# First batch's scale sums as TensorE Gram products, row statistics on ScalarE, idle TensorE slots filled with matmuls, and an offset per operation in the order

## The chip, the cores and the metric

One core of one Trainium2 chip. The metric is the device time of one execution in microseconds (us). The kernel before takes 1000.96 us, the median of three runs (1000.89 to 1001.48).

TensorE is PE in the rows (PEld its weight loads), VectorE is DVE, ScalarE is ACT, GpSimd is POOL, and SyncE is SP, which issues every DMA from one queue.

## The reference

Eight batches of attention with 8 heads, 512 local and 32 global positions of 64 values, then a layer that mixes each batch by a two-dimensional FFT and ends in a feed-forward block:

```python
s_l   = concat([q_l @ k_g.T, where(|i - j| <= 32, q_l @ k_l.T, -1e9)]) / 8
out_l = softmax(s_l) @ concat([v_g, v_l])
out_g = softmax(q_g @ concat([k_g, k_l]).T / 8) @ concat([v_g, v_l])
x  = concat([out_g, out_l]) transposed to (8, 544, 512)
u  = x + real(fft(fft(x, axis=1), axis=2))
un = (u - mean(u)) / sqrt(var(u) + 1e-6)          # over the last axis
out = u + relu(un @ w_ch1) @ w_ch2                # 512 -> 2048 -> 512
```

## The kernel before

The work is cut into jobs. Each `add(engine, us, function, ...)` in `jobs_weights`, `jobs_batch`, `jobs_pair`, `jobs_scores`, `jobs_dft`, `jobs_chunk`, `jobs_mixes` and `jobs_duo` names a job's engine, an assumed length, what it reads and writes, and a due time `t`. The planner `Plan.run` deals the jobs out by due time under the buffers that are free, and `emit` writes them in that order, so that each engine has a fixed list and works through it in order. An engine whose next instruction waits lets nothing behind it pass.

Four kinds of work share the engines:

- **Pairs of heads**, 32 of them, four to a batch (p = 0 to 3 are batch 0). A pair's q, k and v (`load`, `load_v`) are scaled by powers of two that come from sums of their absolute values: `sums` and `sums_v` on ACT, one product with a 128x128 matrix that adds over partitions (`total` in `z_total`), then `z_scale` and `scales` on DVE. `prep_mul` (ACT) scales q and k in place, `prep_hi` (ACT) and `prep_lo` (POOL) split them into two fp16 parts; `v_mul`, `v_hi`, `v_lo` do so for v. Then come, for four units a pair, the scores (PE), a masked copy that also gives the maximum (DVE), exponentials (`exps`) and their two fp16 parts `p_hi` (ACT) and `p_lo` (POOL), a transpose by DMA (`turn`), `values` (PE) and `norm` (DVE), which writes X.
- **The transform of a batch.** `x_square` and `g_square` (ACT) sum the absolute values of X, and `total`, `dft_scale`, `dft_inv` turn that into scales `dsc`. `d_even`, `d_odd` and `d_tail` fold X, and `d_tail_hi`, `d_hi`, `d_lo` split it (tiles ht and eh). `d_first` (PE) is the product along one axis and `d_z`, `d_z2` split its result; `d_second` is the product along the other axis, and `d_add`, `d_addc` and `d_tadd` add it to X.
- **Chunks of 256 rows** through the feed-forward block, c = 0 to 16. `l_bn` takes means and variances, `l_v` turns them into the factors `ve`, `l_hi`, `l_un` and `l_lo` normalise and split, and the rows are turned round: chunk 0 by PE (`l_flip`, 16 matmuls against an identity) and copies (`l_put`) into uh. `f_first` is 24 matmuls of 256 columns, `f_second` 12 of 512.
- **Weights**, 32 loads of 512 KB. `w_low` and `w_split64` and then `w_size` unpack one into a tile, `w_sum` (PE) multiplies its upper halves by themselves, `w_max`, `w_norm` and `w_scale` draw a power of two out of that, and `w_hi` (ACT) and `w_lo` (DVE) split the tile with it.

All weights and all of batch 0, transform and layer norm included, must be through before the first `f_first`. From there on the feed-forward block of one chunk runs while later batches go through attention and transform. Two dictionaries decide what goes first at the start: `FAST` puts batch 0's transform and chunk 0 ahead of other work by a bonus, and `ALOW = 4` gives one `w_low` in four to ACT, the others to POOL.

## Time and profile before

| | before |
|---|---|
| median of three runs | 1000.96 us |
| the profiled execution | 1000.05 us |
| its span, from the first instruction to the last | 998.1 us |
| mean granted TensorE clock over the span | 0.948 |
| PE busy | 906.3 us (91%) |
| DVE, ACT, POOL busy | 725.2, 632.0 and 584.9 us |
| first matmul of the first `f_first` | 139.11 us |

A clock of 1.00 is 2.4 GHz and one of 0.50 is 1.2 GHz. The durations below are from the profiled execution. Busy shares are means over stages that have different limits, so the table alone doesn't say what a change is worth.

### The profile page before, as it was taken

Reading aid. Unit: us, or ns where it says so; the run is one execution under the profiler, and the core shown is the slowest. Engines: PE = TensorE matmul, PEld = TensorE weight load, DVE = VectorE, ACT = ScalarE, POOL = GpSimd, SP = SyncE. Lnnn points to the kernel's source line nnn. Section 1 sums busy time; section 2 is a strip of 40 time slices with the busy share of each in tenths; the row PEclk is TensorE's granted clock in tenths of the full one; section 3 lists DMA queues with packets and bytes.
Section 4 is the critical chain, followed back from the end, with each engine's and each line's share of the span. In section 5 each row is a group of like instructions: output and inputs, shape, how many; then the busy total and the mean of one; then the engine's idle time right before and its main releaser. Section 6 shows DMA issues by size and latency. Waiting matters only on the chain.

```text
span 998.1 us, 24488 instructions
## 1 busy us (share of the span) xinstructions
PE 906.3 (91%) x9352; PEld 631.3 (63%) x9352; DVE 725.2 (73%) x1913; ACT 632.0 (63%) x1353; POOL 584.9 (59%) x860
## 2 busy tenths in 40 slices
PE   1444369999999999999999999999999999999996
PEld 1333347766776767667776676777777666666663
DVE  3788788888757875788578767978775788854543
ACT  6996779967787767666866778576663435421110
POOL 5897468765694658457845875478367266940000
PEclk9665569999999999999999999999999999999998
DMA  9899456735874576368554663668273123201001
GB/s 352 278 254 198 141 128 116 158 98 87 172 141 109 113 132 145 81 134 123 146 95 97 134 165 72 126 115 136 41 130 51 43 51 70 48 6 43 1 1 43
DMA packets 228529, 114.13 MB, mean 114 GB/s; under 512 B 201372, under 2 KB 211004, under 8 KB 228412
## 3 DMA queue, kind: packets, MB, share of 16 engines
q1 hardware_dynamic: 228412, 112.57, 51.3%
q8 instruction: 73, 1.20, 0.5%
q14 instruction: 44, 0.36, 0.1%
HBM read 48.97 MB, written 9.44 MB: 59 GB/s over the span
## 4 chain that ended last, share of the span: by engine, by line
PE 84%; ACT 4%; DMA 4%; DVE 3%; POOL 2%; issue 1%; SPq 1%; DVEq 0%; POOLq 0%; ACTq 0%
PE ps L1088 28%; PE acc L1107 27%; PE bk L1239 7%; PE ps L1306 4%; PE acc L1306 4%; PE bk L632 4%; PE bk L677 2%; PE bk L680 2%; PE bk L959 2%; DMA rw<-in_moe_w_ch 2%; PE bk L924 1%; DMA vf<-in_v 1%; PE bk L706 1%; ACT junk L537 1%; PE bk L742 1%
## 5 line engine op out<-in xcount | busy, mean ns | idle before, releaser
L1088 PE MATMUL ps<-uh,wh 128*128 128x256 f16 x2496 | 290.8, 274 | 0.8 <-ACT uh L1062 0.5
L1107 PE MATMUL acc<-wh,h 128*128 128x512 f16 x1248 | 285.9, 379 | 0.0
L1088 PEld LDWEIGHTS <-wh 128*128 128x128 f16 x2496 | 240.1, 98 | 38.8 <-issue 4.0
L1107 PEld LDWEIGHTS <-h 128*128 128x128 f16 x1248 | 117.1, 98 | 129.7 <-issue 4.4
L656 POOL TENSOR_TENSOR ph<-pe,ph 128x448 f16<-128x448 f32 (+1 forms) x128 | 142.4, 1123 | 82.1 <-ACT ph L651 72.3
L1097 DVE SCALAR_TENSOR_TENSOR h<-ps,h 128x512 f16<-128x512 f32 x104 | 71.5, 687 | 96.9 <-ACT h L1093 96.4
L1093 ACT ACTIVATE h<-ps 128x512 f16<-128x512 f32 x104 | 61.8, 594 | 112.0 <-PE ps L1088 104.4
L647 ACT ACTIVATE pe<-pe,nm 128x224 f32<-128x224 f32 (+1 forms) x256 | 106.1, 475 | 17.5 <-DVE nm L640 17.2
L640 DVE CUSTOM_DVE_ANT_0 pe<-bk,msk,z 128x224 f32<-128x224 f32 (+1 forms) x256 | 101.9, 454 | 12.7 <-PE bk L632 10.4
L651 ACT ACTIVATE ph<-pe 128x448 f16<-128x448 f32 (+1 forms) x128 | 72.2, 579 | 12.1 <-DMA pl<-ph 9.7
L677 PE MATMUL bk<-vN,pl 128*128 128x65 f16 x768 | 64.9, 199 | 7.0 <-DMA pl<-ph 7.0
L677 PEld LDWEIGHTS <-pl 128*128 128x128 f16 x768 | 57.9, 101 | 15.8 <-DMA pl<-ph 10.2
L445 PE MATMUL wl<-wm 128*128 128x128 bf16 x128 | 18.0, 285 | 50.2 <-DVE wm L435 49.2
L618 POOL TENSOR_TENSOR kT<-qk,kT 128x655 f16<-128x655 f32 x32 | 46.3, 1447 | 24.0 <-ACT kT L613 20.7
L680 PEld LDWEIGHTS <-pl 96*128 96x128 f16 (+1 forms) x768 | 55.9, 102 | 3.9
L592 POOL TENSOR_TENSOR vN<-vf,vN 128x640 f16<-128x640 f32 x32 | 45.0, 1406 | 22.5 <-ACT vN L588 11.8
L581 POOL TENSOR_TENSOR vf<-vf,z 128x640 f32<-128x640 f32 x32 | 40.7, 1271 | 22.1 <-DVE ge L543 12.0
L632 PE MATMUL bk<-kT,qT 64*128 64x224 f16 (+2 forms) x960 | 53.4, 255 | 0.3 <-DVE nm L640 0.3
L1288 ACT ACTIVATE hb<-ph 128x512 f16<-128x512 f32 x16 | 10.1, 630 | 66.8 <-DVE ph L1273 66.8
L680 PE MATMUL bk<-vB,pl 96*128 96x65 f16 (+1 forms) x576 | 49.9, 199 | 0.0
L603 ACT ACTIVATE qk<-qk,z 128x655 f32<-128x655 f32 x64 | 46.5, 768 | 0.7 <-DVE z L543 0.7
L537 ACT ACTIVATE junk<-qk 128x512 f16<-128x512 f32 x64 | 43.9, 686 | 3.6 <-DMA qk<-in_qk 2.3
(262 smaller groups left out, 1830.2 us busy)
## 6 DMA issues: line engine op xcount, KB each, us to landing
qk<-in_qk SPq DMA_DIRECT2D x32, 583.5 KB
rw<-in_moe_w_ch SPq DMA_DIRECT2D x22, 512.0 KB
vf<-in_v SPq DMA_DIRECT2D x32, 320.0 KB
out<-X SPq DMA_DIRECT2D x13, 512.0 KB
raw<-in_moe_w_ch SPq DMA_DIRECT2D x10, 512.0 KB
vB<-vN SPq DMA_DIRECT2D x96, 32.5 KB
vB<-vN SPq DMA_DIRECT2D x32, 65.0 KB
pl<-ph SPq DMA_TRANSPOSE x128
```

The lines of the kernel that those rows point to most:

```text
L632: nc.tensor.matmul(S[h][:, t + w0:t + w1], qT[r, a, j], kT[r, KW * c + k0:KW * c + k0 + w1 - w0], start=m == 0, stop=m == 2)
L640: nc.vector.tensor_tensor_reduce(self.per[j][:, h, 0:w], S[h][:, t:t + w], self.msk[:, j, 0:w], z[:, 8:9], 3e38, op0=ALU.add, op1=ALU.min, ...
L647: self.nc.scalar.activation(pe[:, h], pe[:, h], AF.Exp, bias=nm[:, h:h + 1], scale=-1.0)
L651: self.nc.scalar.activation(ph[:, 0, :, 0:WIDE[i % 4]], self.per[i % 4][:, :, 0:WIDE[i % 4]], AF.Copy)
L656: self.nc.gpsimd.tensor_sub(ph[:, 1, :, 0:w], self.per[i % 4][:, :, 0:w], ph[:, 0, :, 0:w])
L677: nc.tensor.matmul(pv[:, j % 2, h], pl[:, 4 * a + 2 * h], vN[:, j, c, h, :], start=m == 0, stop=False)
L680: nc.tensor.matmul(pv[:, j % 2, h], pl[0:n, 4 * a + 2 * h + 1], vb, start=False, stop=m == 2)
L1088: nc.tensor.matmul(ps[:, q], wt[:, w, c0:c0 + P], uh[:, :, 4 * a + kt, :], start=n == 0, stop=n == 11)
L1097: self.nc.vector.scalar_tensor_tensor(h[:, 1], self.fps.pop((c, fp)), 0.0, h[:, 0], op0=ALU.max, op1=ALU.subtract)
L1107: nc.tensor.matmul(self.acc_f[c][j], h[:, a, q, j * P:(j + 1) * P], self.w[1, f][:, w, :], start=f == 0 and a == 0 and w == 0, stop=f == 1 ...
L1239: nc.tensor.matmul(ps, w[x], a[:, :, k * y + o + kt, :], start=m == 0, stop=m == 5)
L1306: nc.tensor.matmul(self.acc_f[c][j], h[:, a, q, j * P:(j + 1) * P], self.w[1, f][:, w, :], start=first and q + a + w == 0, stop=last and q ...
```

## The change

Seven edits, of which the last moves work on all engines.

1. For batch 0 the sums of absolute values on ACT go. `gram` multiplies the upper halves of q, k and v by themselves on PE, 15 matmuls of 128 columns for each of the four pairs, and `gram_max` (DVE) takes the largest entry of each row; `root_of` draws the scale from that, as `w_scale` does for the weights.
2. For pairs 0 and 2 (`DIRECT`) the scaling pass goes: ACT's `prep_hi` and `v_hi` scale while they round, and DVE's `low_of` takes over the low parts of k, q and v from POOL.
3. `ALOW = 2`: every second `w_low` is ACT's. Four `w_lo` go from DVE to POOL in two steps each (`LOP`).
4. The first two operations of `l_v` go from DVE to ACT; the third stays on DVE as `l_m`.
5. `warm` jobs, matmuls of 512 columns on constants whose result nobody reads, are planned from 99 us on wherever PE has nothing else, up to the first `f_first`.
6. Chunk 0's first `l_flip` writes to another PSUM buffer, the last weight sum takes a bank, batch 0's `d_tail` another scratch tile, and `f_first` no longer waits for the end of all weight sums.
7. `OFF`, 149 numbers, is added to due times by operation and by batch, and the planner's constants change.

```diff
+DIRECT = (0, 2)
+OFF = {
+        "b0b_hi": -19.9, "b0b_lo": 2.0, "b0b_mul": -1.2, "b0b_sum": -4.5, "b0d_add": 9.5, "b0d_addc": -2.3, "b0d_first": 9.4, "b0d_hi": -2.1,
...
-ALOW = 4
-LOP = ()
+ALOW = 2
+LOP = (6, 14, 29, 31)
-WARM = ()
-L_HOLD = 81.469
+WARM, WARM_AT = 130, 99.125
+L_HOLD = 105.291
...
+    def gram(self, p):
+        s, pb = self.st[p], self.bank(("bank", "gm", p))
+        for n, f in enumerate((s["q"], s["k"], s["vf"].rearrange("p a b d -> p (a b d)"))):
+            f = f.bitcast(BF16).rearrange("p (n t) -> p n t", t=2)[:, :, 1]
+            at = [*range(0, f.shape[1] - P, P), f.shape[1] - P]
+            for i, o in enumerate(at):
+                self.nc.tensor.matmul(pb[:, P * n:P * n + P], f[:, o:o + P], f[:, o:o + P], start=i == 0, stop=i == len(at) - 1)
...
+        self.nc.vector.tensor_reduce(self.acc[p // 2 % 2][:, n:n + 3], pb, axis=EX, op=ALU.max)
...
+    def root_of(self, r, v):
+        ve, r = self.nc.vector, r.bitcast(I32)
+        ve.tensor_scalar(r, v.bitcast(I32), -0.5, RSQRT, op0=ALU.mult, op1=ALU.add)
+        ve.tensor_scalar(r, r, EXPO, None, op0=ALU.bitwise_and)
...
+    def low_of(self, lo, f, s, hi):
+        self.nc.vector.scalar_tensor_tensor(lo, f, s, hi, op0=ALU.mult, op1=ALU.subtract)
...
-        nc.vector.tensor_scalar(v, mv[:, :, 1], 1e-6, 1.0 / 16.0, op0=ALU.add, op1=ALU.mult)
-        nc.vector.tensor_scalar(y.bitcast(I32), v.bitcast(I32), -0.5, 1597463007.0, op0=ALU.mult, op1=ALU.add)
-        nc.vector.scalar_tensor_tensor(ve[:, 2], mv[:, :, 0], -1.0, y, op0=ALU.mult, op1=ALU.mult)
+        nc.scalar.activation(v, mv[:, :, 1], AF.Copy, scale=1.0 / 16.0, bias=1e-6 / 16.0)
+        nc.scalar.activation(y.bitcast(I32), v.bitcast(I32), AF.Copy, scale=-0.5, bias=1597463007.0)
+
+    def l_m(self, c):
+        mv, ve = self.L[c]["mv"], self.L[c]["ve"]
+        self.nc.vector.scalar_tensor_tensor(ve[:, 2], mv[:, :, 0], -1.0, ve[:, 1], op0=ALU.mult, op1=ALU.mult)
...
     def warm(self, n):
-        self.nc.tensor.matmul(self.bank(("bank", "wm", n)), self.c1[:, 0, 0, 0:P], self.c2.rearrange("p a b c d -> p (a b c d)")[:, 0:512], start=True, stop=True)
+        if n == 0:
+            self.wps = self.ps.tile([P, 512], F32, name="wps", tag="acc1")
+        self.nc.tensor.matmul(self.wps, self.c1[:, 0, 0, 0:P], self.c2.rearrange("p a b c d -> p (a b c d)")[:, 0:512], start=True, stop=True)
...
+        for n in range(WARM):
+            add("PE", .24, self.warm, n, r=[("const",)] + ([] if n else [("ws", 1, 1)]), t=1e6, hold=WARM_AT, margin=.05)
...
-            add("PE", 2.65, self.f_first, c, fp, r=[uh, ("wend",)] + w1, w=[ps], t=t, back=False, margin=.3)
+            add("PE", 2.65, self.f_first, c, fp, r=[uh] + w1, w=[ps], t=t, back=False, margin=.3)
...
+            j.t += OFF.get(j.tag + n, 0.0)
```

What the planner makes of it shows in the engines' lists. Ahead of the first `f_first` PE's list grows from 722 matmuls to 903: 60 of `gram`, 109 of `warm`, and 12 scores that stood behind it; behind it the lists hold the same matmuls but for those scores. Three places matter below.

On ACT, at batch 0's transform, before: L802 is the last x_square and L794 g_square, L537 are sums of batch 1, five of them ahead of the first split of the transform (L897 is d_tail_hi, L874 d_hi).

```order
L783 ACTIVATE X<-xg 32x64 x4
L537 ACTIVATE junk,vac_68<-qk 128x512
L802 ACTIVATE junk,vax_70<-X 128x256
L794 ACTIVATE junk,vax_70<-xg 128x128
L537 ACTIVATE junk,vac_68<-qk 128x655
L537 ACTIVATE junk,vac_68<-vf 128x640
L537 ACTIVATE junk,vac_68<-qk 128x512
L537 ACTIVATE junk,vac_68<-qk 128x655
L897 ACTIVATE ht<-et,dsc 32x513 x2
L874 ACTIVATE eh<-e_1281,dsc 128x514
```

The same place now (L448 and L455 unpack the last weight, L864 is x_square, L856 g_square, L959 d_tail_hi, L936 d_hi, L579 the sums):

```order
L845 ACTIVATE X<-xg 32x64 x4
L448 ACTIVATE ps_1451<-rw 128x512
L448 ACTIVATE ps_1477<-raw 128x512
L455 ACTIVATE lw<-raw 128x512
L864 ACTIVATE junk,vax_70<-X 128x256
L856 ACTIVATE junk,vax_70<-xg 128x128
L959 ACTIVATE ht<-et,dsc 32x513 x2
L936 ACTIVATE eh<-e_1317,dsc 128x514
L579 ACTIVATE junk,vac_68<-qk 128x512
L579 ACTIVATE junk,vac_68<-qk 128x655
```

The sums of batch 1 moved behind the two splits, and the unpacking of the last weight now stands between the copies of the global rows and x_square.

On DVE, from the layer norm's statistics to the first copy into uh, before (L1023 to L1025 are `l_v`, L1030 `l_un`, L1040 `l_lo`, L985 `d_addc`, L1060 `l_put`; masked copies L640 left out):

```order
L1018 BN_AGGR mv<-bst 128x2
L1023 TENSOR_SCALAR ve<-mv 128x2
L1024 TENSOR_SCALAR ve<-ve 128x2
L1025 SCALAR_TENSOR_TENSOR ve<-mv,ve 128x2
L1030 TENSOR_SCALAR un<-X,ve 128x512 x2
L1040 TENSOR_TENSOR unh<-un,unh 128x512 x2
...
L985 SCALAR_TENSOR_TENSOR X<-bk_121,dsc,X 128x2x128 x4
L976 SCALAR_TENSOR_TENSOR X<-bk_123,dsc,X 128x2x128 x2
L1060 COPY uh<-bk_122 128x512
```

And now (L1047 is `d_addc`, L1090 `l_m`, L1054 `d_tadd`, L1125 `l_put`; masked copies L702 left out):

```order
L1080 BN_AGGR mv<-bst 128x2
L1047 SCALAR_TENSOR_TENSOR X<-bk_122,dsc,X 128x2x128 x4
L1090 SCALAR_TENSOR_TENSOR ve<-mv,ve 128x2
L1095 TENSOR_SCALAR un<-X,ve 128x512 x2
L1105 TENSOR_TENSOR unh<-un,unh 128x512 x2
...
L1125 COPY uh<-ps_1857 128x512
L1054 SCALAR_TENSOR_TENSOR xt<-bk_123,dsc,xt 32x2x128 x4
L1125 COPY uh<-flt 128x512
```

Two of `l_v`'s rows are ACT's now, four `d_addc` moved ahead of the third, and four `d_tadd` stand between the two copies.

On PE, from batch 0's last values to `d_first`, before (L472 is `total`, of batch 0's X and of batch 1's first sums; L924 `d_first`):

```order
L680 MATMUL bk_123<-vN,pl 128x65
L472 LDWEIGHTS parth
L472 MATMUL bk_122<-vax_70,parth 128x7
L472 LDWEIGHTS parth
L472 MATMUL bk_121<-vac_68,parth 128x7
L924 LDWEIGHTS eh
L924 MATMUL bk_124<-c1r,eh 128x144
```

And now (L1422 is `warm`; 12 of them stand ahead of the `total`, and 28 between it and `d_first`, L986):

```order
L1422 MATMUL wps<-c2r,c1r 128x512
L497 LDWEIGHTS parth
L497 MATMUL bk_121<-vax_70,parth 128x7
L1422 LDWEIGHTS c1r
L1422 MATMUL wps<-c2r,c1r 128x512
...
L986 LDWEIGHTS eh
L986 MATMUL bk_122<-c1r,eh 128x144
```

The second `total` moved behind the even half of `d_first`, and the fillers came in front of `d_first` instead. Further runs of them stand before `d_second` (11 and 5, then 13), before the scores and `l_flip` (16 and 6) and before the last scores (8). On SP the last weight's load now stands behind the last transposes of batch 0 instead of ahead of them.

## Rows read from the trace of the kernel before

**Rows 1.** Windows by stage: start:end, length, busy us of each engine, clock, DMA share.

```profile
0.00:139.74 139.74, 57.66 (x723) 42.28 (x724) 101.46 (x286) 113.90 (x239) 98.98 (x135) 0.66 0.78 232
...
250.00:360.00 110.00, 110.00 (x1274) 77.94 (x1271) 83.07 (x242) 84.14 (x183) 74.89 (x115) 1.00 0.66 132
...
690.00:800.00 110.00, 110.00 (x1178) 78.37 (x1177) 81.01 (x212) 57.58 (x116) 56.26 (x81) 1.00 0.36 64
```

**Rows 2.** Waits of PE after 139 us: total, times, longest.

```profile
PE ps L1088 <- ACT uh L1062: 0.5, 1, 0.5
```

**Rows 3.** Windows of the stage ahead of the first f_first.

```profile
70.00:90.00 20.00, 11.79 (x203) 9.11 (x203) 18.18 (x55) 18.78 (x43) 18.00 (x23) 0.62 0.75 163
90.00:100.00 10.00, 2.72 (x33) 2.14 (x33) 6.84 (x19) 2.95 (x7) 5.59 (x9) 0.50 1.01 226
```

**Rows 4.** Timeline of SP's queue: start, length, line.

```profile
93.81 6.13 SPq L661 DMA_TRANSPOSE pl<-ph  x2
```

**Rows 5.** Timeline of ACT, with the idle time before a row in brackets.

```profile
98.85 0.62 ACT L422 ACTIVATE ps<-rw 128x512 f32<-128x512 f32 x1 [3.40 <-DMA rw<-in_moe_w_ch]
...
104.25 0.63 ACT L537 ACTIVATE junk<-qk 128x512 f16<-128x512 f32 x1 [1.90 <-DMA qk<-in_qk]
```

**Rows 6.** Groups of ACT to 106 us, shapes apart: busy, mean ns, idle before.

```profile
L429 ACT ACTIVATE lw<-rw 128x512 int32<-128x512 uint32 x6 | 3.9, 652 | 0.0
...
L603 ACT ACTIVATE qk<-qk,z 128x655 f32<-128x655 f32 x4 | 3.3, 828 | 0.0
...
L537 ACT ACTIVATE junk<-qk 128x655 f16<-128x655 f32 x4 | 3.0, 752 | 0.1
...
L537 ACT ACTIVATION_READ_ACCUMULATOR junk<-qk 128x1 f32 x9 | 1.7, 187 | 0.0
```

**Rows 7.** Groups of DVE to 139.7 us, shapes apart.

```profile
L481 DVE SCALAR_TENSOR_TENSOR wh<-wm,wsc,wh 128x512 f16<-128x512 f32 x18 | 18.2, 1021 | 4.0 <-ACT wh L488 4.0
...
L711 DVE TENSOR_REDUCE ng<-bk 128x1 f32<-128x497 f32 x2 | 1.3, 664 | 0.0
```

**Rows 8.** Timeline of DVE: w_scale's first row, last norm, dft_inv, d_lo.

```profile
103.41 0.16 DVE L456 TENSOR_SCALAR mx<-wl 128x1 int32<-128x1 int32 x1 [0.40 <-PE wl L451]
...
105.21 0.42 DVE L693 TENSOR_TENSOR X<-bk,dn 128x256 f32<-128x256 f32 x1
...
108.94 0.15 DVE L546 TENSOR_SCALAR dsc<-dsc 128x1 int32<-128x1 int32 x1
...
113.14 0.75 DVE L878 SCALAR_TENSOR_TENSOR eh<-e,dsc,eh 128x514 f16<-128x514 f32 x1 [0.75 <-ACT eh L874]
```

**Rows 9.** Timeline of ACT: d_tail_hi of batch 0.

```profile
110.89 1.47 ACT L897 ACTIVATE ht<-et,dsc 32x513 f16<-32x513 f32 x2
```

**Rows 10.** Timeline of PE: the total ahead of d_first.

```profile
113.88 0.17 PE L472 MATMUL bk<-vac,parth 128*128 128x7 bf16 x1 [6.99 <-ACT junk L537]
```

**Rows 11.** Timeline of DVE: l_v's first two rows, last l_put, chunk 1's l_v.

```profile
128.75 1.10 DVE L1023 TENSOR_SCALAR ve<-mv 128x2 f32<-128x2 f32 x1
129.88 1.17 DVE L1024 TENSOR_SCALAR ve<-ve 128x2 int32<-128x2 int32 x1
...
139.27 0.42 DVE L1060 COPY uh<-flt 128x512 f16<-128x512 f16 x1
...
141.54 0.17 DVE L1024 TENSOR_SCALAR ve<-ve 128x2 int32<-128x2 int32 x1
```

**Rows 12.** Timeline of PE: first f_first, then scores.

```profile
139.74 4.29 PE L1088 MATMUL ps<-uh,wh 128*128 128x256 f16 x23 [0.26 <-DVE uh L1060]
143.97 0.75 PE L632 MATMUL bk<-kT,qT 64*128 64x224 f16 x12
```

**Rows 13.** Timeline of PE: a later f_first and an f_second.

```profile
157.65 2.79 PE L1088 MATMUL ps<-uh,wh 128*128 128x256 f16 x24
...
161.05 2.76 PE L1107 MATMUL acc<-wh,h 128*128 128x512 f16 x12
```

**Rows 14.** Window of half a microsecond in the first f_first.

```profile
143.50:144.00 0.50, 0.50 (x7) 0.27 (x7) 0.00 (x0) 0.00 (x0) 0.00 (x0) 1.00 1.04 236
```

More of the change, by code (lines that the diff above doesn't have):

```diff
@@ L281, in run @@
             j.start = s
+            going = going or j.fn.__name__ == "f_first"
+            if going and j.fn.__name__ == "warm":
+                j.us = 0.0
             free[e] = s + j.us
@@ L1400, in jobs_scores @@
             x = .05 if nm == "k" else 0
+            if p in DIRECT:
+                add("ACT", .55 + x, self.prep_hi, p, nm, r=[z, o, qk], w=[d])
+                add("DVE", .75 + 4 * x, self.prep_lo, p, nm, r=[z, o, qk, d], w=[d])
+                continue
             add("ACT", .63 + x, self.prep_mul, p, nm, r=[z, o, qk], w=[o])
@@ L1484, in jobs_dft @@
         et, ht = ("et", b), ("ht", b)
[L1485 removed]
+        add("POOL", 4.1, self.d_tail, b, r=xtg, w=[et, ("un" if b else "unh", "st", b)], k=[xt])
         eh = [("eh0", b), ("eh1", b)]
@@ L1525, in jobs_chunk @@
             add("DVE", .86, self.l_bn, c, j, r=r0[j:j + 1], w=[("mv", c)], k=[X], t=L, back=LNB)
-        add("DVE", 1.05, self.l_v, c, r=[("mv", c)], w=[ve], t=L, back=LNB)
+        add("ACT", .40, self.l_v, c, r=[("mv", c)], w=[ve], t=L, back=LNB)
+        add("DVE", .50, self.l_m, c, r=[("mv", c), ve], w=[ve], t=L, back=LNB)
         for j in range(2):
@@ L1579, in jobs_duo @@
                 add("DVE", .86, self.l_bn, c, j, r=[("uj", c, j)], w=[("mv", c)], k=[X], t=L, back=False)
-            add("DVE", 1.05, self.l_v, c, r=[("mv", c)], w=[ve], t=L, back=False)
+            add("ACT", .40, self.l_v, c, r=[("mv", c)], w=[ve], t=L, back=False)
+            add("DVE", .50, self.l_m, c, r=[("mv", c), ve], w=[ve], t=L, back=False)
         end = [("xM", 31), ("xgo", 7, 1)]
```

144 lines of the change are left out of this document (85 added, 59 removed), and 19 rows, old and new, of the table OFF.

## The prediction

> **What bounds the kernel now.** I read the windows by stage first. From the first `f_first` on PE has no gap: its busy time equals the length of the five windows from 250 to 800 us (110.00 of 110.00 in the first and the last of them) at full clock [rows 1], and the longest wait that PE shows after 139 us is 0.5 us [rows 2]. So the span is three pieces laid end to end: the time to the first `f_first` (139.11 us, in the table), some 849 us of matmuls that nothing holds up, and a short end. A cheaper operation on DVE, ACT or POOL after 139 us gives nothing. A microsecond off the first piece is a microsecond off the whole.
>
> In the first piece PE is busy 57.7 of 139.7 us and the other three 99 to 114 [rows 1]. Until 90 us they are nearly full: 18.2, 18.8 and 18.0 of 20 us from 70 to 90, with the DMA at 0.75 of full; from 90 to 100 they drop to 6.8, 3.0 and 5.6 while the DMA stands at 1.01 [rows 3]. That is two limits in turn, work first and then transfers. SP hands over batch 0's last two transposes at 93.81 and is held 6.13 us by them [rows 4]; ACT waits 3.40 us for a weight at 98.85 and then 1.90 us for batch 1's first q and k [rows 5]. The last norm of batch 0 ends at 105.21 + 0.42 = 105.63 [rows 8], which I call N. From N to the first `f_first` there are 33.5 us in which one engine waits for the next, and the clock on PE is at its half level: 0.50 from 90 to 100 [rows 3] and still 23 matmuls in 4.29 us in the first `f_first`, where later 24 take 2.79 [rows 12, 13].
>
> **The change, part by part.** I sum against the profiled execution, 1000.05 us, and add the 0.91 us by which the median lies above it.
>
> **A, work ahead of N.** ACT loses twelve sums at 0.75 + 0.19 us (the rows of a sum overlap a little: 10 us in all) and four scalings (0.83 for k, by columns 0.65 for q: 3.0) and takes seven `w_low` at 0.65 (4.6) [rows 6], so 8.4 us less. POOL loses low parts, some products and eight `w_low`. DVE gains. Four `gram_max` of 384 columns cost 0.51 each by 0.664 us for 497 columns [rows 7]. `low_of` costs between 0.75 us for 514 columns with POOL idle [rows 8] and 1.02 us for 512 in the same form while POOL works [rows 7]; over eight calls of 655, 512 and twice 320 columns for two pairs that is 5.3 to 7.2 us. Four `w_lo` (4.1) and the last `w_scale` (eight rows like the 0.16 us at 103.41 [rows 8], 1.3) leave it. DVE thus has 2.0 to 3.9 us more ahead of N, and was at 18.2 of 20 in the densest window. PE's 60 extra matmuls are hidden: it was busy under half of this piece.
>
> The 1.02 us against 0.75 us is one place where the Trainium skill speaks against this change. "SBUF — State Buffer", section "Who interferes with whom", says that a VectorE instruction with two SBUF inputs contends with a GpSimd instruction that reads SBUF. `low_of` has two such inputs, and by that rule all eight calls would cost the upper figure; the rows agree with it in the one pair of durations.
>
> What does N gain? At least nothing: the same bytes go through the same queue, and transfers were the last limit. At most about 8.4 us, ACT's relief, if transfers could all move up. The DMA's own slack caps that: a quarter of the 20 us from 70 to 90, 5.0 us, is room for transfers that come earlier [rows 3]. On top of it `w_scale` no longer stands ahead of the last norm, and the last weight changes places with the last transposes, which brings the transposes forward but puts that weight's unpacking ahead of the last x_square on ACT. Between 0 and 8.4 I take **-4.0**, near the DMA's slack, less 1 us for DVE's extra work.
>
> **B, from N to the first f_first.** Step by step:
> - *To d_first.* Before, it follows a `total` at 113.88 for which PE had waited 6.99 us because of batch 1's sums [rows 10], so at N + 8.25. Now `d_tail_hi` follows `dft_inv`, which ends at 108.94 + 0.15 = N + 3.46 [rows 8]; 1.47 for the tail [rows 9], half of that for `d_hi`, 0.75 for `d_lo` [rows 8] make N + 6.4. But fillers stand in PE's list: 12 ahead of the `total`, 28 behind it. One is 2.76 / 12 = 0.23 us at full clock [rows 13], and twice that at half. The first 12 can start about when the last norm does. The clock rose between 139.11 and 143.5 when PE had no gap (1.00 at 143.5 [rows 14]), so I take the 12 at mixed speed to N + 3.6 and the 28 at 0.23, 6.4 us, to N + 10.0. That is 1.75 us later than before. `d_first`'s first 24 matmuls of 144 columns then take 1.44 us in place of 2.88, worked out from the two clock levels. Sum +0.3; bounds -3.3 (fillers hidden) and +8.4 (all 40 at half clock, with `d_first` too: N + 18.1 less 8.25, and 1.4 back where the wait was for other engines).
> - *The odd half* of `d_first`, 16 matmuls, at full clock: -1.0; bounds 0 and -1.5 with `d_second`.
> - *w_scale* moves here, onto DVE ahead of `d_add` and the statistics: +1.3; nothing if DVE waits there anyway.
> - *l_v.* Its first two rows take 1.10 and 1.17 us [rows 11] where the same line takes 0.17 in chunk 1 [rows 11]. Now ACT has them, and DVE does four `d_addc` of 256 columns meanwhile, some 1.7 us by half of 0.75 and a little. -0.6 if that sets the pace, +1.0 if ACT's list, which holds batch 1's splits ahead of `l_v`, is late. I take -0.3.
> - *To the last copy into uh*, which started at 139.27 [rows 11]: between the two halves' low parts and that copy DVE now has the masked copies, one copy and four `d_tadd`; before there were also four `d_addc` and four `d_add` in place of the `d_tadd`. Four rows fewer, 0.4 us each, less what ACT's three sums cost its own copies: -1.2; bounds 0 and -1.7.
>
> Together **-0.9**, bounds -5 and +8.
>
> On `l_v` the Trainium skill speaks against the change a second time: "ScalarE: Activation LUTs", section "Rules for kernel authors", says to use VectorE rather than ScalarE for add and multiply, and to budget about 0.3 us for each activation. By that, two would cost an estimated 0.6 us against 0.34 on a VectorE that nothing disturbs, and the sum would be 0.3 us less good; the 1.10 and 1.17 us of the trace outweigh it in this one place, where the time counts.
>
> **C, the first f_first at full clock.** Its 24 matmuls ran from 139.11 to the scores at 143.97, 4.86 us; later ones take 2.79 [rows 12, 13]. With fillers up to the last moment: **-2.1**, and nothing if the clock falls before it.
>
> **D, twelve scores** (0.75 us [rows 12]) move from behind the first `f_first` to ahead of it, where PE has time: **-0.75**.
>
> Behind that nothing is removed from PE: 0. All matmuls there are the same, in another order. What covers it is the room that the other engines have (83 of 110 us on DVE, 84 on ACT [rows 1]); without that cover, every late operand is a gap.
>
> Sum: -4.0 - 0.9 - 2.1 - 0.75 = -7.75 on 1000.05, so 992.3, and by the median 993.2 us, **0.8% faster**.
>
> **The rivals.**
> 1. *N doesn't move.* The transfers were the last limit at 90 to 100 us [rows 3], their bytes are unchanged, and DVE gets more work. Then A is nothing or at most the 0.6 us of `w_scale`, and the time is 993.2 + 3.6 = 996.8. Against it: ACT was at 18.8 of 20 when the DMA had a quarter free. Chance 0.24.
> 2. *The fillers become the bound (slower).* A filler is not skipped when real work is ready. If the clock stays at half through the 40 around the `total`, they last 18.4 us where about 6.7 are free, `d_first` starts at N + 18.1, and C is lost with it: B is +8, so -4.0 + 8 - 0.75 = +3.3, 1004.2. It decides from the point where B passes +4.8. For it: 0.50 in every window of this stage. Against: the clock did rise within 4.4 us of matmuls without a gap. Chance 0.09.
> 3. *PE gets gaps behind 143 us.* New due times move every operation, and one chunk's un or one batch's transposes arriving late shows as a wait where there was 0.5 us. The engines' lists have room in the mean, but order decides. To eat the gain takes 7.75 us of gaps; a few us, hence about 998, are likelier than that. Chance 0.13, of which a third slower than before.
> 4. *Both limits ahead of N give way* and B comes to its good bound: -8 - 3 - 2.9, about 987. Chance 0.08.
>
> My own forecast, 990 to 996, has 0.46. Changes under 0.2% (2 us) can't be told from none here. Slower than that: most of rival 2 and a third of rival 3, 0.13. Same: 0.08, from what is left of rivals 1 to 3 near 1000. Faster: 0.79. The range that leaves 2 in 10 out is 987.0 to 1000.5 us.
>
> **What the new profile would show.** Right, if the last norm ends near 101.6, the granted clock is 1.00 before the first `f_first`, this starts near 134.2 and its 24 matmuls take under 3 us, and the windows behind stay at 110.00 of 110.00. A is wrong if ACT waits longer for weights or DVE's row before the last norm is late on `low_of`; B is wrong if PE runs fillers while eh or z is long ready; C is wrong if the clock is 0.50 at `f_first`. PE waits after 140 us that sum to more than 1 us would show rival 3.

## The result, and the profile after

The changed kernel takes 1006.15 us (median of five runs, 1005.04 to 1008.21) against 1000.96 for the kernel before (five runs beside them, 998.63 to 1001.48): a ratio of 1.0057 [1.0039, 1.0074]. It is **slower by 0.6%**, where 0.8% faster was predicted, and lies outside the range. The span of the profiled execution grew by 6.4 us, from 998.1 to 1004.6.

The stage ahead of the first `f_first` did get shorter. Windows of the changed kernel by the same stages as [rows 1], the first up to the first `f_first`:

```profile
0.00:136.03 136.03, 83.59 (x903) 55.58 (x903) 105.96 (x296) 106.35 (x217) 85.12 (x121) 0.84 0.83 237
250.00:360.00 110.00, 109.66 (x1279) 77.14 (x1277) 87.17 (x243) 83.13 (x186) 75.01 (x110) 1.00 0.72 136
690.00:800.00 110.00, 110.00 (x1148) 78.37 (x1147) 72.77 (x200) 49.15 (x106) 33.89 (x57) 1.00 0.31 62
```

`f_first` starts 3.08 us earlier, POOL is down from 99 to 85 us of this stage, and the two long windows behind are nearly as full as before (109.66 and 110.00 of 110). Here is the start itself, in the timeline of PE (compare [rows 12]):

```profile
136.03 5.41 PE L1153 MATMUL ps<-uh,wh 128*128 128x256 f16 x48
```

48 matmuls in 5.41 us are 2.7 per 24: full clock from the first one. What the predicted gain went into shows in the waits of PE behind this point. The kernel before had one of 0.5 us there [rows 2], and two of 0.3 and 0.2. The four longest now (total, times, longest):

```profile
PE acc L1172 <- DVE wh L506: 3.0, 2, 2.4
PE ps L1371 <- DVE hb L1358: 1.9, 1, 1.9
PE bk L694 <- POOL qT L680: 0.9, 1, 0.9
PE bk L694 <- POOL kT L680: 0.7, 1, 0.7
```

The first, third and fourth lie together, at 157 to 168 us; the second is one wait at 864 us. Where time was gained and lost, I read from the two traces with a count of my own: the columns of the matmuls that each kernel still has ahead of it at one and the same time (fillers left out), divided by 2.4 GHz, so in us at full clock. The difference is how far the changed kernel is ahead of the one before. It is good to about 1 us.

| at (us) | 145 | 155 | 160 | 165 | 170 | 175 | 300 | 860 | 880 | end |
|---|---|---|---|---|---|---|---|---|---|---|
| ahead by (us) | 6.5 | 6.0 | 4.9 | 2.1 | -2.1 | -3.4 | -2.9 | -4.3 | -6.4 | -6.3 |

6.5 us were won by 145 us. 9.4 of what was lost went within 20 us, from 155 to 175, and 2.1 at 864. Windows of the first place (in the kernel before PE is busy 5.00 of 5 in each of these four, at clock 1.00):

```profile
155.00:160.00 5.00, 4.46 (x37) 2.24 (x36) 4.21 (x7) 5.00 (x11) 4.88 (x7) 1.00 0.70 143
160.00:165.00 5.00, 3.39 (x33) 1.38 (x30) 5.00 (x1) 2.34 (x6) 5.00 (x5) 0.77 0.57 133
165.00:170.00 5.00, 2.60 (x7) 0.93 (x7) 4.93 (x12) 2.50 (x7) 1.79 (x2) 0.50 1.02 242
170.00:175.00 5.00, 5.00 (x102) 3.84 (x101) 3.85 (x16) 4.12 (x9) 3.02 (x6) 0.71 0.40 47
```

PE is idle for 4.55 of the 20 us, and its clock falls to 0.50: its busy time in each window by what the clock lacks of 1.00 is 0.78 + 1.30 + 1.45 = 3.5 us more. DVE shows one single instruction in the second window. The timeline of DVE has it, the low half of the sixth second-layer weight:

```profile
158.81 0.85 DVE L506 SCALAR_TENSOR_TENSOR wh<-wm,wsc,wh 128x512 f16<-128x512 f32 x1
159.89 7.45 DVE L506 SCALAR_TENSOR_TENSOR wh<-wm,wsc,wh 128x512 f16<-128x512 f32 x1 [0.23 <-ACT wh L513]
```

And POOL at that time, a row without a gap, the low parts of pairs 6 and 7 (L680) and of two units' p (L718):

```profile
159.78 1.42 POOL L680 TENSOR_TENSOR kT<-qk,kT 128x655 f16<-128x655 f32 x1
161.17 1.15 POOL L680 TENSOR_TENSOR qT<-qk,qT 128x512 f16<-128x512 f32 x1
162.28 2.02 POOL L718 TENSOR_TENSOR ph<-pe,ph 128x448 f16<-128x448 f32 x2
164.26 1.42 POOL L680 TENSOR_TENSOR kT<-qk,kT 128x655 f16<-128x655 f32 x1
165.65 1.14 POOL L680 TENSOR_TENSOR qT<-qk,qT 128x512 f16<-128x512 f32 x1
```

The same instruction takes 0.74 us when nothing disturbs it, and 0.78 to 1.86 in the kernel before between 150 and 176. Here it lasts 7.45 us and ends at 167.34, 0.55 us behind POOL's row. `f_second` needs that half and waits 2.41 us; all that is queued behind it on DVE waits too, and ACT waits 5.0 us for this `w_lo`.

### The profile page after: what moved, and what is told of

The parts are those of the page before. It is cut to its first block, busy times and chain, and to the rows that moved or that the text cites. A ratio compares the mean times of both kernels' runs of the same rounds, so it can differ in the third digit from the quotient of the medians.

```text
span 1004.6 us, 24794 instructions
## 1 busy us (share of the span) xinstructions
PE 935.2 (93%) x9521; PEld 645.5 (64%) x9521; DVE 722.4 (72%) x1890; ACT 630.0 (63%) x1367; POOL 577.8 (58%) x852
## 5 line engine op out<-in xcount | busy, mean ns | idle before, releaser
L1172 PE MATMUL acc<-wh,h 128*128 128x512 f16 x1248 | 288.5, 381 | 3.0 <-DVE wh L506 3.0
L718 POOL TENSOR_TENSOR ph<-pe,ph 128x448 f16<-128x448 f32 (+1 forms) x128 | 139.8, 1100 | 98.3 <-ACT ph L713 85.4
L702 DVE CUSTOM_DVE_ANT_0 pe<-bk,msk,z 128x224 f32<-128x224 f32 (+1 forms) x256 | 102.4, 454 | 11.3 <-PE bk L694 10.9
L680 POOL TENSOR_TENSOR kT<-qk,kT 128x655 f16<-128x655 f32 x30 | 43.3, 1444 | 16.8 <-ACT kT L672 15.3
L694 PEld LDWEIGHTS <-qT 64*128 64x128 f16 x960 | 36.4, 99 | 16.1 <-issue 10.9
L645 POOL TENSOR_TENSOR vN<-vf,vN 128x640 f16<-128x640 f32 x30 | 41.8, 1395 | 7.9 <-ACT vN L637 7.0
L1371 PE MATMUL ps<-wh,hb 128*128 128x512 f16 x192 | 44.2, 379 | 1.9 <-DVE hb L1358 1.9
L1371 PE MATMUL acc<-wh,h 128*128 128x512 f16 x192 | 45.8, 379 | 0.0
```

Source lines behind the costliest of these rows:

```text
L694: nc.tensor.matmul(S[h][:, t + w0:t + w1], qT[r, a, j], kT[r, KW * c + k0:KW * c + k0 + w1 - w0], start=m == 0, stop=m == 2)
L702: nc.vector.tensor_tensor_reduce(self.per[j][:, h, 0:w], S[h][:, t:t + w], self.msk[:, j, 0:w], z[:, 8:9], 3e38, op0=ALU.add, op1=ALU.min, ...
L718: self.nc.gpsimd.tensor_sub(ph[:, 1, :, 0:w], self.per[i % 4][:, :, 0:w], ph[:, 0, :, 0:w])
L1172: nc.tensor.matmul(self.acc_f[c][j], h[:, a, q, j * P:(j + 1) * P], self.w[1, f][:, w, :], start=f == 0 and a == 0 and w == 0, stop=f == 1 ...
L1371: nc.tensor.matmul(self.acc_f[c][j], h[:, a, q, j * P:(j + 1) * P], self.w[1, f][:, w, :], start=first and q + a + w == 0, stop=last and q ...
```

## The experiments

Each ratio is against runs of the kernel before beside it; "ahead" is the count of the table, from the profiled execution. Where a kernel has "the tail of before", this is its diff (by itself it brings 1006.15 down to 1003.77, see below, so kernels with it compare with that):

```diff
-PL = 75
-T_AT, T_PACE = 803.116, 12.26
-BOOST = 0
+PL = 39.601
+T_AT, T_PACE = 793.534, 12.914
+BOOST = 12.091
```

### Is it the long w_lo? (pause, no low halves, clock)

**A pause on GpSimd.** POOL's next low part has to wait for that `w_lo`, by a copy of two of its columns:

```diff
+            if at in (("prep_lo", 6, "q"), ("p_lo", 22)):
+                held.append(j)
                 continue
             j.fn(*j.a)
+            if at == ("w_lo", 1, 5, False):
+                k.nc.gpsimd.tensor_copy(k.rest, k.w[1, 5][:, 1, 0:2])
+                for h in held:
+                    h.fn(*h.a)
```

> Changed kernel with one added wait: ahead of the second low part of pair 6 (prep_lo of q), GpSimd first reads two columns that w_lo of the sixth second-layer weight writes, so that GpSimd pauses and VectorE's w_lo (7.45 us there in the changed kernel) can run. Every engine's order is otherwise the same. Theory 1, VectorE was kept off the shared SBUF port by a row of GpSimd instructions with no gap: the w_lo takes under 2.5 us, PE's idle time between 150 and 175 us falls from 6 us to under 1.5, the clock stays at 1.00 there, and the time falls by 7 to 10 us, to 996 to 999 us. Theory 2, the second-layer weights are split too late in the new order, and the f_second would wait for them anyway: the w_lo is shorter but PE waits elsewhere in the same stretch, and the time is 1004 to 1007.

Measured: 1002.64 us, 1.0011 [1.0003, 1.002]. Timeline of DVE and, below it, of POOL:

```profile
159.82 1.87 DVE L517 SCALAR_TENSOR_TENSOR wh<-wm,wsc,wh 128x512 f16<-128x512 f32 x1 [0.22 <-ACT wh L524]
```

```profile
159.72 1.42 POOL L691 TENSOR_TENSOR kT<-qk,kT 128x655 f16<-128x655 f32 x1
161.75 0.18 POOL L350 COPY rest<-wh 128x2 f16<-128x2 f16 x1 [0.61 <-DVE wh L517]
161.89 1.15 POOL L691 TENSOR_TENSOR qT<-qk,qT 128x512 f16<-128x512 f32 x1
```

Same start, 1.87 us in place of 7.45: with POOL's row broken, `w_lo` ends 0.55 us behind the instruction that POOL had in hand. So it is POOL's unbroken row that holds it. The time came only 3.5 us down, not the 7 or more that I expected: ahead is 1.7 at 170, 0.5 at 175 and -2.8 at the end. The pause holds up pair 6's q, for which PE now waits 1.7 us.

**The pause one instruction later** (ahead of `p_lo` alone, with the tail of before):

```diff
-            if at in (("prep_lo", 6, "q"), ("p_lo", 22)):
+            if at == ("p_lo", 22):
```

> Changed kernel with the four constants of the last stage from before, and with GpSimd's pause moved one instruction on: it waits for the sixth second-layer w_lo behind both low parts of pair 6, ahead of p_lo of unit 22, so that the scores which need those low parts are not held up by the pause. Theory 1 (VectorE is kept off the port by GpSimd's row): the w_lo ends at the first gap, near 163 us, and takes 3 us; PE then waits only for the two low parts (0.7 and 0.9 us) and for 0.5 us of an earlier w_lo; PE's lead over the kernel before is 2.5 to 4 us at 175 us where the pause one step earlier left 0.5 and none left -3; time 998.5 to 1001. Theory 2 (PE stands too early at f_second and scores whose operands are late): the lead at 175 us stays between -1 and 1.5, time 1001 to 1003.

1002.06 us, 1.0010 [1.0000, 1.0020]. `w_lo` took 2.98 us and ended once more 0.55 us behind the last POOL instruction ahead of the pause; PE waited 0.9 for q, 0.7 for k and 0.6 for the weight; ahead 1.7 at 170 and 0.5 at 175. The waits traded places.

**And chunk 0's sixth `f_first` moved on PE** (`early`) ahead of the scores that wait for pair 6:

```diff
+            if at == ("scores", 12):
+                early.fn(*early.a)
```

> The kernel of the late pause, and one f_first (the sixth of chunk 0, 2.7 us of PE work whose operands are ready) moved on PE from behind these scores and f_second to ahead of the scores. Theory 2: the wait for pair 6's low parts (1.6 us) is covered, the clock does not fall, and the lead at 175 us is 4.5 to 6 us; time 996 to 999. Theory 1 alone: what is lost was the VectorE lockout, so this adds less than 1 us to the late pause's result.

1002.47 us, 1.0013 [1.0002, 1.0023]. Ahead by 4.2 at 170, nothing lost from 155 until there, but then a later `w_lo` was kept off for 4.08 us from 171.66, and 0.5 was left at 175, -2.3 at 190. That is neither of the two outcomes expected. Repairing one place uncovers the next.

**No low halves.** Every `w_lo` of the second layer is a memset of zeros, which leaves that part of the product out:

```diff
+        if k:
+            self.nc.vector.memset(w[:, 1], 0.0)
+            return
         self.nc.vector.scalar_tensor_tensor(w[:, 1], f, s, w[:, 0], op0=ALU.mult, op1=ALU.subtract)
```

> Changed kernel that leaves out the low halves of the second-layer weights: where VectorE computed one (w_lo), it writes zeros to the same tile, about 0.3 us and with no input from SBUF. Every engine's order is the same. If VectorE's lockouts and the time of these w_lo are the loss behind 155 us: PE waits in 145 to 195 us only for pair 6's low parts (1.6 us or less), the lead at 190 us is 4 to 6 us, and the time is 996 to 999. If PE is ahead of everything there, ScalarE's splits and GpSimd's low parts too: the lead at 190 us is still under 2 us and the time 1000 to 1003.

998.89 us, 0.9979 [0.9969, 0.9990]. Of PE's waits from 145 to 195 us one row is left:

```profile
PE bk L697 <- POOL qT L683: 0.3, 1, 0.3
```

Ahead is 5.6 at 155 and still 4.7 at 175, 4.2 at 300 and 3.1 at 830. With these splits out of the way the lead of the first stage survives; 1.6 us then go at DVE's `hb` again, where PE waits 1.9 us.

**Only the clock.** The scores ahead of the stalled `f_second` are issued four times more, 72 matmuls of added work:

```diff
             j.fn(*j.a)
+            if (j.fn.__name__, *j.a) == ("scores", 12):
+                for _ in range(4):
+                    j.fn(*j.a)
```

> Changed kernel with 72 matmuls more: the 18 matmuls of the scores that stand ahead of the third f_second of chunk 0 are done five times in a row instead of once (same values), 2.9 us of work in the place where PE waits for the locked-out w_lo. The w_lo keeps its 7.45 us and ends near 167.3. If half of what is lost between 155 and 175 us is the clock that falls while PE waits (0.77, 0.50 and 0.71 from 160 to 175): the clock stays at 1.00 there, the lead over the kernel before at 175 us goes from -3.4 to 0 to 1.5 us, and the time falls to 1001.5 to 1003.5 in spite of the added work. If the waits alone cost it: the lead at 175 stays at -3 or gets worse, time 1006 or more.

1004.0 us, 1.0028 [1.0018, 1.0039]: 2.15 us faster than the changed kernel, with more work. `w_lo` is 7.46 us as before. Windows of PE at the stall:

```profile
160.00:165.00 5.00, 3.41 (x93) 3.05 (x91) 4.99 (x1) 2.45 (x6) 5.00 (x5) 1.00 0.59 139
165.00:170.00 5.00, 4.06 (x78) 2.24 (x76) 4.93 (x12) 2.37 (x7) 1.92 (x2) 1.00 1.35 214
```

Here the clock stays at 1.00, and ahead is -1.2 at 175 in place of -3.4 (the added matmuls left out of the count). So some 2 us of the loss were the clock's fall, which this idle time brought with it. That is less than I expected, and the two ratios' intervals just touch: the trace carries this more than the time does.

### What makes DVE stay out? (two measurements by themselves)

A small kernel that writes zeros: DVE's `w_lo` form beside a row of six POOL subtractions like those of L680, at start moments set by a copy of varying width ahead of it.

```diff
+        for _ in range(n):
+            nc.gpsimd.tensor_sub(lo, a, ah)
+        nc.vector.tensor_copy(d[:, 0:cols], pt[:, 0:cols])
+        nc.vector.scalar_tensor_tensor(wh[:, 1], w if two else pw, s, wh[:, 0], op0=ALU.mult, op1=ALU.subtract)
```

> A kernel of its own that computes nothing of the reference (it writes zeros). VectorE runs the w_lo instruction (128x512, two inputs in SBUF) while GpSimd runs six or two 128x512 subtractions without a gap; a copy in front of it starts it at 20 moments spread over half a microsecond against GpSimd's first subtraction, and five times with one of the two inputs in PSUM. Theory 1: at most moments it gets in at GpSimd's next instruction (0.74 to 2 us), at some it waits for the whole row of six (6 us or more), and with two subtractions never over 3 us; with one input in PSUM it takes 0.75 us or a little more at every moment. If a lockout is not a matter of GpSimd's row: no w_lo above 2.5 us.

> The small kernel (zeros as output) with the w_lo started at 41 moments from about 0.9 to 1.5 us behind the start of GpSimd's first of six subtractions, thus from 0.25 us ahead of the start of the second to 0.35 us behind it. The w_lo that took 7.45 us began 0.11 us behind the start of a GpSimd subtraction, one of 4.08 us 0.20 us ahead of one; those that began 0.29 to 0.87 us behind one all got in at the next. If the moment of the start decides: some of these 41 wait for the rest of the row, 5 us or more, in one stretch of the moments; elsewhere 0.8 to 2 us. If something else in the kernel locks it out: all stay under 2.1 us.

The second kernel shifts the start in 41 steps from 0.21 us ahead of a POOL instruction's start to 0.36 behind it. Groups of DVE by shape, first of the one kernel, then of the other (pw is in PSUM):

```profile
L42 DVE SCALAR_TENSOR_TENSOR wh<-w,s,wh 128x512 f16<-128x512 f32 x27 | 29.2, 1083 | 0.0
L42 DVE SCALAR_TENSOR_TENSOR wh<-pw,s,wh 128x512 f16<-128x512 f32 x6 | 4.4, 741 | 0.0
```

```profile
L43 DVE SCALAR_TENSOR_TENSOR wh<-w,s,wh 128x512 f16<-128x512 f32 x41 | 56.6, 1380 | 0.0
```

With both large inputs in SBUF it waits for the POOL instruction in hand and gets in at the next one: up to 1.73 us, and the POOL instruction behind it takes 1.48 in place of 1.15. Where it starts first, 0.05 to 0.21 us ahead of the POOL instruction (8 trials), it takes 0.74 and that instruction 1.53 to 1.70. With one input in PSUM it takes 0.74 always. But in 68 trials, 62 of them beside six POOL instructions, it was never kept out for more than one. So I can say which form is at risk and what frees it, and not what decides between 1.9 and 7.45 us: it isn't the start moment alone. One difference is left untested: POOL's instructions start 1.23 us apart here at 1.15 us of length, which leaves 0.08 us between two, while in the changed kernel each starts before the one ahead has ended (161.17 against 159.78 + 1.42). That can't be all either: in the kernel before, a `w_lo` at 159.55 us got in after 0.99 between two such POOL instructions without a gap. In the kernel the outcome repeats (7.45 to 7.74 us in all six kernels with this order of the two engines there).

### The parts of the change (fillers, sums, w_low, tail)

**No fillers:**

```diff
-            if j.fn.__name__ == "warm" and j.start > t0:
+            if j.fn.__name__ == "warm":
```

> Changed kernel without the 109 warm matmuls, all else in the same order. If the fillers hold the clock and that is worth its keep: the granted clock is 0.5 from 90 us to the first f_first, the transform's matmuls take twice as long, f_first starts at 137 to 139 us instead of 136.0 and its first 24 matmuls take 4.3 us or more, in all a lead smaller by 3 to 5 us at 150 us. If the fillers cost what they give, because real work waits behind them: f_first starts before 136 and the lead at 150 us is within 1 us of the changed kernel's. The time itself also hangs on whether VectorE's long w_lo near 160 us comes again at the shifted moment; without it the time is below 1001.

1005.0 us, 1.0039 [1.0024, 1.0055]. The first `f_first` starts at 135.95, no later than with them (136.03), but its 24 matmuls take 4.49 us in place of 2.80; ahead is 5.2 at 150 in place of 6.2. They buy C, about 1 us net, and that microsecond is lost at 159 us too (`w_lo` 7.74 us).

**Sums on ACT again**: absolute sums at the places of `gram_max` (and of the squares for the global rows), in the order as changed.

```diff
+        return self.sums(p, "q"), self.sums(p, "k"), self.sums_v(p)
...
-        scale = self.scale_of if g > 1 else self.root_of
+        scale = self.scale_of
```

> Changed kernel with batch 0's scale sums as absolute sums on ScalarE again, in the places where gram_max stood, and without the Gram products and the two-step roots. All else in the same order. If ScalarE's relief is what moved the last norm of batch 0 from 105.6 to 103.6 us: it ends near 105.5 again and f_first starts 1.5 to 2.5 us later. If the weights' and transposes' transfers set it: the norm ends within 0.5 us of 103.6 and f_first starts where it did.

1013.62 us, 1.0123 [1.0109, 1.0137]. The last norm of batch 0 ends at 113.02 in place of 103.59 us, 9.4 later; from 70 to 90 us ACT is at 19.46 of 20. So with the sums ACT's work does bound this stage, and the Gram products relieve it. Without them the next run asks what bounds it, and so does the part on A below.

**`w_low` one in four on ACT**, as before, in the order as changed:

```diff
-        if n % ALOW == ALOW - 1:
+        if n % 4 == 3:
```

> Changed kernel with w_low as before (one in four on ScalarE, the others on GpSimd), all in the same order. If ScalarE's work bounds the way to the last norm of batch 0: the norm ends 2 to 4 us earlier than 103.6. If GpSimd does, or the two are even: it ends at 103.6 or up to 4 us later. If the transfers do: within 0.5 us of 103.6.

1004.17 us in one run; last norm at 103.45, so the other `w_low` on ACT cost the norm nothing: ACT is no longer the limit there. Ahead is -2.0 at 175.

**The tail of before** (its diff is above):

> Changed kernel with the four constants of the last stage from before (T_AT, T_PACE, PL, BOOST). The order of every engine is that of the changed kernel up to about 600 us. Theory 1 with a lockout that comes from the order alone: the w_lo near 160 us takes 7 us or more again. If it is chance: under 3 us, and the time falls by 7 to 10 us. For the end: the 1.9 us that PE waits for hb at 864 us is gone and the time is 1 to 3 us less, if the last stage's order brought it; otherwise within 1 us of 1006.

1003.77 us, 1.0024 [1.0013, 1.0035]. `w_lo` 7.46 us again. The time is 2.4 us less than the changed kernel's, as expected if the last stage's order brought the wait; but the wait isn't gone, it falls from 1.9 to 1.2 us, and the loss there only from 2.1 to 1.5.

### Can the splits come earlier? (due times)

Three kernels with the tail of before bring second-layer splits forward: two by `S2_AT`, their first due time, from 182.549 to 140 and to 150, and one by dropping the offset `w1w_scale` (+19.2).

```diff
-S2_AT, S2_PACE = 182.549, 1.5
+S2_AT, S2_PACE = 140, 1.5
...
-            j.t += OFF.get(j.tag + n, 0.0)
+            j.t += (0.0 if j.tag + n in ('w1w_scale',) or j.tag in ('w1w_scale',) else OFF.get(j.tag + n, 0.0))
```

> Changed kernel with the last stage's four constants of before and the due times of the second-layer splits brought forward (S2_AT 140 in place of 182.5), which changes the order of all engines behind 128 us. The second-layer splits then stand ahead of pair 6's and 7's work. If their place was the cause: PE waits for no w_lo between 150 and 195 us, the clock stays at 1.00, the lead over the kernel before at 190 us is 3 to 6 us and the time 997 to 1000. If the stage is too full for the lead whatever the order: the lead at 190 us is under 1.5 us because PE waits for pairs 5 to 7 instead (scores, p, low parts), and the time 1001 to 1004.

> As the run with 140, with 150: the first nine second-layer splits come forward, the others later. Place as the cause: lead 2 to 5 us at 190 us, time 998 to 1001. Stage too full: as there.

> Changed kernel with the last stage's four constants of before and without one entry of the table, the 19.2 us by which the due time of the second layer's scale is put off. If that entry put the splits into pair 6's stretch: the third to tenth w_lo still end by 173 us but apart from GpSimd's rows, PE waits less than 2 us for them, time 998 to 1001. If not: a w_lo of over 4 us again and 1003 to 1006.

1010.52 us, 1.0092 [1.0076, 1.0107]; 1008.81, 1.0076 [1.0061, 1.0091]; 1010.71, 1.0096 [1.0081, 1.0111]. With 140 and 150 PE has no wait from 145 to 195 us at all and is 3.4 and 3.7 ahead at 190. Then it is -9.8 and -5.8 at 300 (the third: 3.8 and -9.1; no `w_lo` is over 2.0 us there, yet PE waits 3.7 us for one that DVE starts only at 188.90). Waits of PE from 235 to 300 us with 140, and the window of the stall:

```profile
PE bk L497 <- ACT junk L579: 4.1, 1, 4.1
PE bk L1021 <- DVE X L1038: 1.7, 1, 1.7
```

```profile
250.00:260.00 10.00, 3.49 (x44) 2.35 (x33) 9.33 (x25) 4.68 (x12) 4.28 (x13) 0.50 0.44 77
```

PE waits there for sums on ACT and for the `d_add` of batch 1 (L1038); DVE is at 9.33 of 10 and the clock at 0.50. Moving the splits only moved the gap. It isn't the sum of DVE's time that is short: from 145 to 260 us DVE is busy 86.7 of 115 us here, and 99.6 in the version with three pauses below, which is still 4.7 ahead at 300. Why batch 1's transform comes late in these orders, I didn't take apart.

**The offsets of batch 0 alone** (all others of `OFF` at zero by the same line, tail of before; the diff stands with the last version below):

> Changed kernel with the last stage's four constants of before and with the offsets of batch 0's operations alone; those of the weights, of batch 1 and later and of the chunks are zero. If the offsets for later work cost time: the slow loss behind 200 us (1 to 1.5 us by 800) is gone. If they are worth their keep: the first f_first comes 1 us or more later and the time is 1005 or more. The w_lo stand in much the same place, so a lockout of over 4 us near 160 us is expected by the theory of the place.

1001.46 us, 1.0003 [0.9993, 1.0013]. The last norm ends at 99.16, 4.4 us earlier than in the changed kernel, and ahead is 7.3 at 155. Then one `w_lo` takes 6.36 us from 157.7 and one 3.03 from 171.0; PE waits 2.8 us for the first and 1.5 for one ahead of it, and 0.1 is left at 175. The wait at 864 us is gone.

### A version that keeps part of the lead

**Pauses behind every second-layer `w_lo` from the third on** (in the kernel with the moved `f_first`, with `w_low` as before):

```diff
+            if at[0:2] == ("w_lo", 1) and not at[3] and at[2] > 1:
+                k.nc.gpsimd.tensor_copy(k.rest, k.w[1, at[2]][:, 1, 0:2])
```

> The kernel of the late pause with the f_first moved ahead, and more: GpSimd reads two columns behind every second-layer w_lo of VectorE from the third on, so that no row of GpSimd can run past one, w_low is split between ScalarE and GpSimd as before, and the last stage's four constants are those of before. If the lockouts are what is left of the loss: no w_lo above 3.2 us, a lead of 3 to 5 us at 190 us and 997 to 1000. If the pauses cost GpSimd what they give: a lead under 1 us and 1001 to 1003.

1001.89 us, 1.0004 [0.9992, 1.0016]. No `w_lo` of this stretch is over 1.91 us, but PE waits 2.2 us for transposes of p, whose low parts POOL makes; ahead is 3.8 at 170, -0.6 at 175, -3.4 at the end. So many pauses, it seems, cost POOL what they give DVE.

**Batch 0's offsets, and three pauses** where a long row of POOL meets a `w_lo` (`wait` names the POOL job and the weight for which it now waits):

```diff
+        wait = {("prep_lo", 7, "k"): 4, ("p_lo", 22): 5, ("p_lo", 25): 8}
...
+                k.nc.gpsimd.tensor_copy(k.rest, k.w[1, i][:, 1, 0:2])
...
-            j.t += OFF.get(j.tag + n, 0.0)
+            j.t += (0.0 if j.tag + n in ('w0', 'w1', 'b1', 'c1', 'b2', 'c2') or j.tag in ('w0', 'w1', 'b1', 'c1', 'b2', 'c2') else OFF.get(j.tag + n, 0.0))
```

> The kernel with the offsets of batch 0 alone, in which a w_lo took 6.36 us at 157.7 and one 3.03 at 171.0, with three pauses of GpSimd: ahead of pair 7's first low part it waits for the fifth second-layer w_lo, ahead of p_lo of unit 22 for the sixth, ahead of p_lo of unit 25 for the ninth. If the lockouts are what loses the first stage's lead there (7.3 us at 155, 0.1 at 175): no w_lo above 2.5 us, the lead at 175 us is 3 to 6 us, and the time 997 to 1000. If batch 1's transform bounds whatever lead is left: a lead of 3 us or more at 190 that is under 1 us at 300, and 1000.5 to 1002.

> The same without warm matmuls. By what the fillers gave in the changed kernel (a lead of 6.2 against 5.2 us at 150 us without them): the lead at 150 us is 1 us smaller, and the time 0 to 1.5 us longer.

The first: **997.46 us (996.84 to 998.02), 0.9957 [0.9945, 0.9969]**, faster than both kernels and leaving nothing out. The pauses are all that parts it from the kernel with batch 0's offsets alone (1001.46): no `w_lo` is over 2.03 us, and they are worth 4.0 us. The same `w_lo` in DVE's timeline, first with batch 0's offsets alone, then with the pauses:

```profile
157.72 6.36 DVE L506 SCALAR_TENSOR_TENSOR wh<-wm,wsc,wh 128x512 f16<-128x512 f32 x1
```

```profile
156.19 1.88 DVE L533 SCALAR_TENSOR_TENSOR wh<-wm,wsc,wh 128x512 f16<-128x512 f32 x1
```

The second, the same without fillers: 996.70, 0.9953 [0.9940, 0.9966]. Waits of PE from 145 to 195 us and the window from 250 to 360 of the first:

```profile
PE acc L1199 <- DVE wh L533: 1.5, 1, 1.5
PE bk L766 <- DMA pl<-ph: 1.0, 1, 1.0
PE bk L831 <- DVE nm L729: 0.4, 1, 0.4
```

```profile
250.00:360.00 110.00, 110.00 (x1291) 77.79 (x1289) 87.41 (x251) 87.31 (x197) 79.08 (x122) 1.00 0.72 141
```

Ahead is 8.9 at 150, 5.1 at 175, 4.7 at 300, 3.0 at 860 and 3.2 at the end. Without fillers it is 7.6 at 150 and 5.3 at 175: the microsecond that they buy is gone by 165 us (7.3 in both), since PE then waits for others anyway.

## Why the prediction was wrong

Step by step, with its names.

**A**, -4.0: measured -2.0 (the last norm at 103.59 against 105.63), and not by the way that A names. ACT's relief was to bring the transfers forward, but batch 0's last transposes go out no earlier. Before:

```profile
95.22 4.73 SPq L661 DMA_TRANSPOSE pl<-ph  x1
```

Now, on SP, PE and DVE:

```profile
95.37 1.70 SPq L723 DMA_TRANSPOSE pl<-ph  x1
102.11 0.19 PE L739 MATMUL bk<-vN,pl 128*128 128x65 f16 x1
101.79 0.69 DVE L461 SCALAR_TENSOR_TENSOR wm<-ps,lw 128x512 int32<-128x512 int32 x1 [1.11 <-ACT ps L448]
102.70 0.22 DVE L753 TENSOR_SCALAR dn<-bk,z 128x4 f32<-128x4 f32 x1 [0.22 <-PE bk L742]
103.17 0.42 DVE L755 TENSOR_TENSOR X<-bk,dn 128x256 f32<-128x256 f32 x1
```

They land at 101.77 us (102.03 before, by the semaphore events of the two traces), with the DMA at 1.17 of full from 90 to 100 us, and PE's last values and the norm follow at once; DVE's wait for a weight (1.11) isn't on this path in this execution. So the transfers are still the last limit and gave 0.3 us. The rest was won behind the landing, where `w_scale` no longer stands ahead of the norm and PE comes to the last values 0.8 us sooner after it. That ACT's work can be the limit holds: with the sums put back the last transposes go out at 103.81 and the norm comes 9.4 us later. Without them the order decides: with batch 0's offsets alone they go out at 91.34, and with the three pauses at 89.68, and the norm ended at 99.16 and 97.57 us, so up to 8 us were there to be had. Between kernels whose lists are the same up to there the norm's time differed by 1.9 us (103.59 to 105.46), so the -2.0 is the best of seven.

**B**, -0.9: measured -1.0 (32.44 us from N to `f_first` against 33.48). `d_first` starts at N + 8.2 (111.78), as before; I had N + 10.0, of which 1.44 us were to come back by faster products. The clock was already 0.94 from 100 to 110 us, where I had counted on half speed at first, and the fillers held `d_first` 1.0 us after its operand was ready at 110.79. ACT's two rows of `l_v` took 0.20 us each, which is less than the 1.10 and 1.17 of [rows 11] and near the 0.17 that the same group shows for chunk 1. The 0.3 us for each that the Trainium skill ("ScalarE: Activation LUTs", "Rules for kernel authors") says to budget, and from which I worked out 0.6 us, are meant for an activation whose bias is a [128,1] operand. Here scale and bias are constants, so that figure was not the one to use.

**C**, -2.1: measured -2.1 (24 matmuls through 2.80 us after the start, 4.92 before). With **D**, -0.75, 48 matmuls were through at 141.45 against 147.44: 6.0 us earlier by then, of the 7.75 of the sum.

**The step that failed** is the next one: "Behind that nothing is removed from PE: 0", with "What covers it is the room that the other engines have (83 of 110 us on DVE, 84 on ACT [rows 1])". That room is a mean over a window of 110 us that starts at 250 us; it says nothing of a single wait, nor of the stretch right behind the gain. PE, 6 us ahead, comes to the second-layer weights and to pairs 6 and 7 before DVE and POOL are done with them. In the kernel before the other engines kept up, but with little to spare: DVE is busy 16.9, ACT 18.1 and POOL 16.7 of the 20 us from 155 to 175. The term is not 0 but +12.8: +9.4 from 155 to 175 us, +2.1 at 864, and the rest in small pieces.

**Rival 3** named this (gaps behind 143 us, order decides), with a chance of 0.13 and a price of a gap that was too low: "To eat the gain takes 7.75 us of gaps" left out that the clock can fall with a gap. From 155 to 175 us 4.55 us of idle time went with a loss of 9.4, and the clock fell to 0.50; at 864 us a wait of 1.9 cost 2.1, and the clock stayed at 1.00. The rival also looked for a late chunk or transpose; it was a weight's split on DVE. **Rival 1** was right in its ground, that the transfers are the last limit, but N moved all the same, and it doesn't explain a longer time. **Rival 2** is out: the fillers cost 1 us at one place and gave 2 at another. Its "0.50 in every window of this stage" misreads [rows 3], which has 0.62 from 70 to 90 us.

Of the 9.4 us lost from 155 to 175, the runs show these parts, which overlap: the `w_lo` kept off by POOL's row (3.9 us come back at 175 when that row is broken), the clock (2.2 when it is held), and all splits of the second layer together (8.1 when DVE is spared them). The plainest price of POOL's rows is that of the version with three pauses: they take the lead at 175 from 0.1 to 5.1 and the time from 1001.46 to 997.46. That one freed instruction isn't enough in the changed kernel's order shows in the runs with one pause, where the next wait follows.

The wait at 864 us is DVE's first `hb` (the low part of a hidden layer in the last stage), and there the order is what changed. Before, it starts at 856.93, ahead of four rows of DVE with two SBUF inputs (`s_mix`, from 860.05); in the changed kernel it stands behind them, at 864.49, and they take 1.22, 1.37, 1.37 and 0.83 us (0.43, 0.41, 0.41 and 1.27 before), with POOL busy 5.00 of 5. With the tail of before it is still behind them, and PE waits 1.2; with batch 0's offsets alone it is ahead of them, and the wait is gone. That POOL lengthens these rows too looks likely, but no run broke its row there.

What stays open is why this `w_lo` is kept out for a whole row of POOL instructions when others get in at the next. The Trainium skill ("SBUF — State Buffer", "Who interferes with whom") says that a VectorE instruction with two SBUF inputs contends with a GpSimd instruction that reads SBUF, and that issue order decides who blocks. The small kernels agree with the first part (0.74 us with an input in PSUM, 1.08 and 1.38 on average without), and with the second in that whichever started first kept the other waiting for one instruction. The wait for a row of six, as it stands in the changed kernel, isn't explained by that, and the small kernels didn't make one.
